# Splitting the second expert matrix into two parts, one tile ahead

## The chip, the cores and the metric

One core of a Trainium2 chip runs the whole program. Times are device microseconds (us) of that core; several runs of the same program give a median. One execution was recorded by the hardware profiler, and all rows of the trace come from it.

## What is computed

Attention with a block mask (4 x 8 heads, 576 tokens, 64 wide) gives x of 2304 tokens by 512. A dense layer follows, and then a layer of 8 experts, in which each token goes to one expert or to none. What matters here is that last layer:

```python
def _moe2_ref(x, w_skip, w_gate, w1, w2):
    do_compute = x @ w_skip > 0
    out = x.copy()
    xc = x[do_compute]
    logits = xc @ w_gate
    e_idx = np.argmax(logits, axis=1)
    ...
    for e in range(E):          # E = 8, w1[e] is 512 x 1024, w2[e] is 1024 x 512
        mask = e_idx == e
        h = np.maximum(xc[mask] @ w1[e], 0.0)
        y[mask] = gate_w[mask, None] * (h @ w2[e])
    out[do_compute] = xc + y
```

## The kernel before

Attention comes first, the dense layer overlaps its end, and the expert layer is the last stage. Tokens are sorted by expert into lists in DRAM. A tile is 128 tokens of one expert: their rows are gathered, turned by TensorE (turn_x, L881), multiplied with the expert's first matrix (two halves of 512 columns, four chunks of rows each), passed through relu (ScalarE), turned again (turn_h), multiplied with the second matrix (8 chunks of rows, summed in one bank, py), scaled and added to x by VectorE (finisher, L966 to L974: the tile yo) and scattered to the output by GpSimd. The number of tokens decides at run time how many tiles an expert has: further tiles stand in nested conditional blocks (tc.If, L1132), and expert 7 stands in one as a whole (L1117). The instructions of a block are ordered by a scheduler that lists what is ready by its own estimate of time; each engine then works in that order. tc.keep_in_program_order puts an instruction behind the one that was written before it on the same engine.

Two forms of product are in use. Expert 0 (expert_tile, L926) has its weights and its inputs split into a rounded part (hi, type float32r) and the rest (lo), and computes a product as three: hi*hi, hi*lo, lo*hi (products, L893). ScalarE or VectorE makes the rounded part, VectorE or GpSimd subtracts (split_piece, L859). The raw weights come in pieces of 128 rows by 512 columns through places of the pool CV (raw holds two pieces, cv2 and cv3 one, three places each), 12 pieces ahead (load_piece, L842). Experts 1 to 7 (expert_tile32, L976) multiply float32 with float32 directly: mm1 at L984, mm2 at L987, the copy of turned h at L997. Their two matrices are loaded by SP into one of four pairs of places (load_expert, L816), up to four experts ahead. Expert 0's first tile is computed early, beside the routing of the last tokens; its second (the call with filled, L1131) follows at about 700 us, while SP loads the lists of all experts (L1093 to L1096).

Of the kernel before, what the change touches and what calls it, by code (L numbers as in the profile page):

```python
# [346 lines left out]
def attention_moe_kernel(  # L347
# [468 lines left out]
    def load_expert(e):  # L816

        if e >= E:
            return
        k_ = (e - 1) % 4  # L820
        if k_ < 3:
            x, y = ((wo_at[0], wo_at[1]), (wi_at[2], wo_at[2]), (wi_at[0], wi_at[1]))[k_]
            a, b = ((WA if t < 2 else WB).tile([128, 2, 4 * 512], F32, name=f"wbt{t}").rearrange("p i w -> p (i w)") for t in (x, y))
            a, b = a.rearrange("p (c w) -> p c w", w=F2), b.rearrange("p (c k w) -> p c k w", k=2, w=D)
        else:
            a, b = (C.tile([128, ND, HALF], F32, name=f"xT{i}") for i in range(2))
            a, b = a[:, :, 0:F2], b[:, :, 0 : 2 * D].rearrange("p c (k w) -> p c k w", k=2)
        for c in range(ND):
            nc.sync.dma_start(a[:, c], w1[e, c * 128 : (c + 1) * 128])
        for c in range(ND):  # L830
            nc.sync.dma_start(b[:, c], w2[e, c * 256 : (c + 1) * 256].rearrange("(k p) w -> p k w", p=128))
        weights[e] = [a[:, c] for c in range(ND)], [b[:, f // 2, f % 2] for f in range(NF2)]

# [65 lines left out]
    def places(own=False):  # L899

        bank = lambda nm, *shape: ps3.tile([128, *shape], F32, name=nm, tag="ps")
        return dict(hh=M3.tile([128, NF2, 128], F32R, name="hh", bufs=1),
                    hl=M3.tile([128, NF2, 128], F32R, name="hl", bufs=1),
                    ph=[bank("ph3", 512) for _ in range(2)],
                    py=psx.tile([128, 512], F32, name="py", bufs=1) if own else bank("py", 512),
                    pt=lambda: bank("pt", 4, 128), hs=lambda f: M3.tile([128, 512], F32, name="hs"),
                    yo=lambda: M3.tile([128, 512], F32, name="yo"))

# [16 lines left out]

    def expert_tile(lx, ahead=(), at=None, begin=run_all, between=None):  # L926

# [19 lines left out]
        begin(m1[0])  # L947
        relu(0)
        run_all(m1[1][:9] if between else m1[1][:7])
        if between:  # L950
# [5 lines left out]
        turn_h(1)  # L956
        run_all(m2[4:7])
        if between:
            between[1]()
# [15 lines left out]

    def expert_tile32(e, hw, lx, ahead=(), at=None):  # L976

        a, b = weights[e]
        at = at or places()
        ph, py = at["ph"], at["py"]  # L980
        h = {}

        def mm1(f, c):
            tc.keep_in_program_order(nc.tensor.matmul(ph[f], lx["xw"][:, c], a[c][:, f * 512 : f * 512 + 512], start=(c == 0), stop=(c == ND - 1)))  # L984

        def mm2(f):
            tc.keep_in_program_order(nc.tensor.matmul(py, hw[:, f], b[f], start=(f == 0), stop=(f == NF2 - 1)))  # L987

        def relu(f):
            h[f] = at["hs"](f)  # L990
            nc.scalar.activation(out=h[f], in_=ph[f], func=AF.Relu)

        def turn_h(f):
            pt = at["pt"]()
            for c in range(4):
                tc.keep_in_program_order(nc.tensor.transpose(pt[:, c], h[f][:, c * 128 : (c + 1) * 128], ident))
            nc.vector.tensor_copy(hw[:, 4 * f : 4 * f + 4], pt)  # L997

        for c in range(ND):
            mm1(0, c)  # L1000
        relu(0)
        for c in range(2):
            mm1(1, c)
        turn_h(0)
        for c in range(2, ND):
            mm1(1, c)
        relu(1)
        for f in range(2):
            mm2(f)
        turn_h(1)  # L1010
        for f in range(2, 6):
            mm2(f)
        run_all(ahead)
        for f in range(6, NF2):
            mm2(f)
        return finisher(lx, at, py)
# [76 lines left out]
    with tc.issue_after(end.ins):  # L1093
        for k_ in (2, 1, 0, 3):
            load_lists(lall[k_], lambda l: l.rearrange("(e n) c -> n e c", e=E)[k_ * 128 : (k_ + 1) * 128], nc.sync)
            find(lall[k_])  # L1096
    for e in (1, 2):
        load_expert(e)
    p2.close()
# [3 lines left out]
    xgs.insert(4, xgf[1])  # L1103
    xts = [[M3.tile([128, ND, 128], F32R, name=f"xt{i}{j}", bufs=1) for j in range(2)] for i in range(2)]
    xts = [xtf[0], xts[0], xtf[1], xts[1]]
    fourth = lane(lall[3], 0, xgs[0], xts[2])
    xws = [CV.tile([128, ND, 128], F32, name=nm, bufs=3) for nm in ("cv2", "cv2", "cv3", "cv3")]
    hw = [CV.tile([128, NF2, 128], F32, name="raw", bufs=3) for _ in range(2)]
    firsts = [lane32(lall[0], e, xgs[e % 4], xws[e % 2]) for e in range(E)]
    for lx in (firsts[1], fourth, firsts[2], firsts[3]):  # L1110
        gather(lx)
    for e in range(E):
        ahead1 = [lambda: turn_x(firsts[e + 1])] if e + 1 < E else []
        some = ExitStack()
        if e:
# [3 lines left out]
            gather(second)  # L1119
            finish = expert_tile32(e, hw[0], firsts[e], ahead1, at=places(True))  # L1120

# [5 lines left out]

        tile_of = (lambda *a: expert_tile32(e, hw[1], *a)) if e else expert_tile

        def more(k_, lx):  # L1130
            filled = e == 0 and k_ == 1  # L1131
            with nullcontext() if filled else tc.If(nreg[e] > 128 * k_):  # L1132
                if k_ == 1 and not filled:
                    turn_x(lx)
                if k_ < KS:
                    ahead = []
                    nx = later(k_ + 1)
                    if k_ + 1 < KS:
                        if nx is not fourth:
                            gather(nx)  # L1140
                        ahead = [lambda: turn_x(nx)]
                    finish = tile_of(lx, ahead + (ahead1 if filled else []))
                    finish()
# [50 lines left out]
```

## Time and profile before

| | us |
|---|---|
| median of 3 runs | 867.64 (866.53 to 868.01) |
| the profiled execution, its own time | 869.34 |
| span from first to last instruction in it | 867.6 |
| TensorE busy in the span | 799.5 (92%) |
| VectorE, ScalarE, GpSimd busy | 524.2, 399.0, 354.0 |

The profile names the engines PE (TensorE products), PEld (TensorE's loading of the fixed operand, which overlaps), DVE (VectorE), ACT (ScalarE), POOL (GpSimd) and SP (the engine that issues most transfers); a q behind the name is the engine's sequencer. A row of the timeline gives start, duration, engine, line of the kernel, operation, tile written<-tiles read and a count; in brackets stand the idle time before it and what ended it. "issue" there means that nothing the profile shows was waited for. Both types of product are called f32 in it.

### The profile page before, as it was taken

How to read it: one execution, taken by the hardware profiler on the slowest of the kernel's cores; microseconds unless marked ns; L12 is line 12 of the kernel's file. 1: busy time of each engine (PE TensorE's matmuls, PEld its weight loads, DVE VectorE, ACT ScalarE, POOL GpSimd, SP SyncE). 2: the span in 40 equal slices, each digit the busy share in tenths (PEclk: the TensorE clock that was granted, in tenths of full speed). 3: DMA queues.
4: the chain of work that ended last, by engine and by line, in shares of the span. 5: the costliest groups of instructions: out<-in, count | busy, mean ns of one | idle time of the engine just before them, and what ended most of it. 6: DMA issues, size and time to landing. Idle time of an engine off the chain costs nothing. (4 is left out here: it accounts for less than half of the span.)

```text
span 867.6 us, 12388 instructions
## 1 busy us (share of the span) xinstructions
PE 799.5 (92%) x4100; PEld 657.4 (76%) x4100; DVE 524.2 (60%) x1122; ACT 399.0 (46%) x909; POOL 354.0 (41%) x427
## 2 busy tenths in 40 slices
PE   6688999989999999987999999999999979989995
PEld 4577787979888788876899888898998758544442
DVE  6786888877968984489719798558222722111111
ACT  5786887877778774565422222222232412101110
POOL 3665554453545564455432544423315341010210
PEclk9899999999999998998999999999999989999998
DMA  6564753474341143543521523113036761693920
GB/s 168 138 180 109 192 124 82 108 190 129 72 106 42 40 165 121 167 156 130 169 73 73 170 69 128 37 73 110 3 116 206 271 95 37 230 398 140 320 60 7
DMA packets 114653, 112.89 MB, mean 130 GB/s; under 512 B 76718, under 2 KB 79790, under 8 KB 114562
## 3 DMA queue, kind: packets, MB, share of 16 engines
q1 hardware_dynamic: 106386, 95.72, 36.4%
q0 software_dynamic: 8176, 16.06, 6.2%
q8 instruction: 44, 0.72, 0.3%
q14 instruction: 47, 0.39, 0.1%
HBM read 81.23 MB, written 22.70 MB: 120 GB/s over the span
## 5 line engine op out<-in xcount | busy, mean ns | idle before, releaser
L438 PE MATMUL ph<-xT,wbt 128*128 128x384 f32 x864 | 168.7, 342 | 0.7 <-ACT cv L480 0.7
L438 PEld LDWEIGHTS ph<-xT,wbt 128*128 128x128 f32 x864 | 155.2, 191 | 8.4 <-ACT cv L480 1.1
L430 POOL TENSOR_TENSOR gl<-u,gh 128x384 fp32r<-128x384 f32 x72 | 80.2, 1115 | 154.3 <-ACT gh L429 129.5
L438 PE MATMUL acc<-wbt,gh 128*128 128x512 f32 x432 | 133.3, 398 | 7.6 <-ACT cv L405 4.9
L185 POOL TENSOR_SCALAR P<-P,stat 128x128 f32<-128x128 f32 (+2 forms) x144 | 78.9, 568 | 76.4 <-DVE stat L183 54.6
L429 DVE TENSOR_TENSOR u<-ph,u 128x384 f32<-128x384 f32 x72 | 39.6, 550 | 97.4 <-ACT u L428 94.7
L438 PEld LDWEIGHTS acc<-wbt,gh 128*128 128x128 f32 x432 | 80.0, 188 | 21.1 <-ACT cv L405 5.1
L429 ACT CAST gh<-u 128x384 fp32r<-128x384 f32 x72 | 36.9, 512 | 104.7 <-PE acc L438 49.3
L438 PE MATMUL acc<-wbt,gl 128*128 128x512 f32 x216 | 82.1, 396 | 0.0
L428 ACT ACTIVATE u<-ph 128x384 f32<-128x384 f32 x72 | 35.2, 489 | 83.1 <-PE ph L438 75.2
L285 PE MATMUL pv<-ph,vs 128*128 128x320 f32 (+4 forms) x280 | 70.7, 323 | 2.7 <-DVE ph L239 1.6
L161 PE MATMUL sp<-wbt 128*128 128x128 f32 (+2 forms) x192 | 58.2, 382 | 12.4 <-DMA wbt<-wbt 4.9
L236 PE MATMUL pt<-ident,P 128*128 128x128 f32 x400 | 62.6, 283 | 6.2 <-ACT P L174 2.5
L438 PE MATMUL ph<-xT,wia 128*128 128x384 f32 x288 | 58.9, 351 | 3.4 <-DVE cv L429 2.1
L409 POOL TENSOR_TENSOR cv<-cv,cv 128x512 int32<-128x512 int32 x32 | 45.5, 1424 | 32.7 <-DVE cv L408 21.8
L285 PEld LDWEIGHTS pv<-ph,vs 128*128 128x128 f32 x280 | 51.2, 192 | 8.9 <-DVE ph L239 2.5
L438 PE MATMUL po<-woa,gA 128*128 128x512 f32 x216 | 56.4, 407 | 0.5 <-ACT cv L480 0.5
L648 DVE CUSTOM_DVE_ANT_0 xlast<-x,raw 128x512 f32<-128x512 f32 x72 | 56.7, 834 | 0.0
L236 PEld LDWEIGHTS pt<-ident,P 128*128 128x128 f32 x400 | 47.0, 143 | 11.9 <-ACT P L174 3.1
L438 PEld LDWEIGHTS ph<-xT,wia 128*128 128x128 f32 x288 | 51.7, 196 | 4.5 <-DVE cv L429 2.4
L243 DVE TENSOR_TENSOR pl<-pt,ph 128x512 fp32r<-128x512 f32 (+2 forms) x84 | 50.9, 624 | 5.2 <-ACT ph L242 4.2
L438 PEld LDWEIGHTS po<-woa,gA 128*128 128x128 f32 x216 | 41.2, 195 | 9.0 <-ACT cv L480 0.9
(244 smaller groups left out, 1537.7 us busy)
## 6 DMA issues: line engine op xcount, KB each, us to landing
wbt<-in_moe_w_dram SPq DMA_DIRECT2D x48, 512.0 KB, 6.9
wbt<-wbt SPq DMA_DIRECT2D x60, 144.0 KB, 2.5
raw<-in_moe_w_in_dram SPq DMA_DIRECT2D x16, 512.0 KB, 4.1
raw<-in_moe_w_out_dram SPq DMA_DIRECT2D x16, 512.0 KB, 3.7
xTd<-xT POOLq DMA_DIRECT2D x4, 1152.0 KB, 8.0
part_d<-cv SPq DMA_DIRECT2D x18, 256.0 KB, 2.1
x<-part_d SPq DMA_DIRECT2D x6, 768.0 KB, 4.6
xT<-xTd POOLq DMA_DIRECT2D x6, 768.0 KB, 6.9
```

The source lines that it names most:

```text
L161: nc.tensor.matmul(o_, st()[a][h][:, rows : rows + m], st()[b][:, h, c : c + w], start=(i == 0), stop=(i == 1))
L185: nc.gpsimd.tensor_scalar(out=P, in0=P, scalar1=rs[:, i : i + 1], scalar2=1.0, op0=ALU.mult, op1=ALU.mult)
L236: nc.tensor.transpose(o, src, self.ident)
L243: nc.vector.tensor_tensor(out=dl, in0=s_, in1=dh.bitcast(F32), op=ALU.subtract)
L285: nc.tensor.matmul(box["pv"][:, c0:N], v, box[t][:, i, h, cs], start=(jc == 0 and t == "ph"), stop=(jc == runs[-1][0] and t == parts[-1]))
L409: nc.gpsimd.tensor_tensor(out=w, in0=w, in1=low, op=ALU.add)
L428: nc.scalar.activation(out=u, in_=ph, func=AF.Copy, scale=0.01)
L429: return [nc.vector.tensor_tensor(out=u, in0=ph, in1=u, op=ALU.max), nc.scalar.copy(gh, u), nc.gpsimd.tensor_tensor(out=gl, in0=u, in1=gh. ...
L430: nc.gpsimd.tensor_tensor(out=gl, in0=u, in1=gh.bitcast(F32), op=ALU.subtract)]
L438: nc.tensor.matmul(ps, x, y, start=first and m == 0, stop=last and m == 3 * n - 1)
L648: nc.vector.tensor_tensor_reduce(out=junk, in0=x2[:, t], in1=wrow[j], scale=1.0, scalar=0.0, op0=ALU.mult, op1=ALU.add, accum_out=box["L"] ...
```

## The change

The second matrix of experts 1 to 7 is split like expert 0's. Its raw pieces come through the places of CV, 12 pieces ahead (load_later), and are split during the first tile of the expert before (split_later), a few in four places of that tile, eight in expert 0's second tile for expert 1. The split matrix goes to one of two places in turn: the third pair of the dense layer's weights for odd experts, expert 0's own place for even ones. load_expert now loads the first matrix alone, into one of four places. In the tile, h is split as in expert 0 (ScalarE copies, VectorE subtracts), and the second matrix takes 24 products instead of 8. The first stays float32. The turned x gets places of its own, since CV's are taken, and the result yo has one place instead of two.

```diff
--- before.py
+++ after.py
@@ -817,19 +817,44 @@
 
         if e >= E:
             return
-        k_ = (e - 1) % 4
-        if k_ < 3:
-            x, y = ((wo_at[0], wo_at[1]), (wi_at[2], wo_at[2]), (wi_at[0], wi_at[1]))[k_]
-            a, b = ((WA if t < 2 else WB).tile([128, 2, 4 * 512], F32, name=f"wbt{t}").rearrange("p i w -> p (i w)") for t in (x, y))
-            a, b = a.rearrange("p (c w) -> p c w", w=F2), b.rearrange("p (c k w) -> p c k w", k=2, w=D)
-        else:
-            a, b = (C.tile([128, ND, HALF], F32, name=f"xT{i}") for i in range(2))
-            a, b = a[:, :, 0:F2], b[:, :, 0 : 2 * D].rearrange("p c (k w) -> p c k w", k=2)
+        t = (wo_at[0], wo_at[1], wi_at[0], wi_at[1])[(e - 1) % 4]
+        a = (WA if t < 2 else WB).tile([128, 2, 4 * 512], F32, name=f"wbt{t}").rearrange("p i w -> p (i w)").rearrange("p (c w) -> p c w", w=F2)
         for c in range(ND):
             nc.sync.dma_start(a[:, c], w1[e, c * 128 : (c + 1) * 128])
-        for c in range(ND):
-            nc.sync.dma_start(b[:, c], w2[e, c * 256 : (c + 1) * 256].rearrange("(k p) w -> p k w", p=128))
-        weights[e] = [a[:, c] for c in range(ND)], [b[:, f // 2, f % 2] for f in range(NF2)]
+        if e % 2:
+            b = [wbt[t].rearrange("p i (f w) -> p (i f) w", w=D) for t in (wi_at[2], wo_at[2])]
+            b = [[x[:, f] for f in range(NF2)] for x in b]
+        else:
+            b = w2buf
+        weights[e] = [a[:, c] for c in range(ND)], b
+
+    later_raws = {}
+
+    def load_later(i):
+
+        e, f = divmod(i, NF2)
+        e += 1
+        if e >= E:
+            return
+        nm = tags[i % AHEAD]
+        n = 2 if nm == "raw" else 1
+        t = CV.tile([128, n, 512], F32, name=nm, bufs=3)
+        for k_ in range(n):
+            later_raws[i + k_] = t[:, k_]
+        nc.sync.dma_start(t, w2[e, f * 128 : (f + n) * 128, :].rearrange("(n p) w -> p n w", p=128))
+
+    def split_later(e):
+
+        def step(f):
+            i = (e - 1) * NF2 + f
+            (hi, lo), r = (x[f] for x in weights[e][1]), later_raws.pop(i)
+            tc.keep_in_program_order(nc.scalar.copy(hi, r))
+            nc.vector.tensor_tensor(out=lo, in0=r, in1=hi.bitcast(F32), op=ALU.subtract)
+            nm = tags[i % AHEAD]
+            if nm != "raw":
+                load_later(i + AHEAD - (nm is None))
+
+        return [lambda f=f: step(f) for f in range(NF2)] if e < E else []
 
 
     tags = ("raw", None, "cv2", "cv3") * 3
@@ -904,7 +929,7 @@
                     ph=[bank("ph3", 512) for _ in range(2)],
                     py=psx.tile([128, 512], F32, name="py", bufs=1) if own else bank("py", 512),
                     pt=lambda: bank("pt", 4, 128), hs=lambda f: M3.tile([128, 512], F32, name="hs"),
-                    yo=lambda: M3.tile([128, 512], F32, name="yo"))
+                    yo=lambda: M3.tile([128, 512], F32, name="yo", bufs=1))
 
     def places_early():
 
@@ -923,7 +948,7 @@
                     pt=lambda: bank("acc1", 4, 128),
                     yo=lambda: CV.tile([128, 512], F32, name="cv2", bufs=3))
 
-    def expert_tile(lx, ahead=(), at=None, begin=run_all, between=None):
+    def expert_tile(lx, ahead=(), at=None, begin=run_all, between=None, fill=()):
 
         a, b = w1buf, w2buf
         at = at or places()
@@ -946,6 +971,7 @@
 
         begin(m1[0])
         relu(0)
+        run_all(fill[:4])
         run_all(m1[1][:9] if between else m1[1][:7])
         if between:
             between[0]()
@@ -955,6 +981,7 @@
         run_all(m2[:4])
         turn_h(1)
         run_all(m2[4:7])
+        run_all(fill[4:])
         if between:
             between[1]()
         run_all(m2[7:18])
@@ -973,18 +1000,16 @@
 
         return finish
 
-    def expert_tile32(e, hw, lx, ahead=(), at=None):
-
-        a, b = weights[e]
+    def expert_tile32(e, lx, ahead=(), at=None, fill=()):
+
+        a, (bh, bl) = weights[e]
         at = at or places()
-        ph, py = at["ph"], at["py"]
-        h = {}
+        ph, py, hh, hl = at["ph"], at["py"], at["hh"], at["hl"]
+        m2 = products(py, [(hh[:, c], hl[:, c]) for c in range(NF2)], list(zip(bh, bl)))
+        h, fill = {}, list(fill)
 
         def mm1(f, c):
             tc.keep_in_program_order(nc.tensor.matmul(ph[f], lx["xw"][:, c], a[c][:, f * 512 : f * 512 + 512], start=(c == 0), stop=(c == ND - 1)))
-
-        def mm2(f):
-            tc.keep_in_program_order(nc.tensor.matmul(py, hw[:, f], b[f], start=(f == 0), stop=(f == NF2 - 1)))
 
         def relu(f):
             h[f] = at["hs"](f)
@@ -994,25 +1019,31 @@
             pt = at["pt"]()
             for c in range(4):
                 tc.keep_in_program_order(nc.tensor.transpose(pt[:, c], h[f][:, c * 128 : (c + 1) * 128], ident))
-            nc.vector.tensor_copy(hw[:, 4 * f : 4 * f + 4], pt)
-
+            nc.scalar.copy(hh[:, 4 * f : 4 * f + 4], pt)
+            nc.vector.tensor_tensor(out=hl[:, 4 * f : 4 * f + 4], in0=pt, in1=hh[:, 4 * f : 4 * f + 4].bitcast(F32), op=ALU.subtract)
+
+        def some():
+            run_all(fill[:2])
+            del fill[:2]
+
+        some()
         for c in range(ND):
             mm1(0, c)
         relu(0)
+        some()
         for c in range(2):
             mm1(1, c)
         turn_h(0)
         for c in range(2, ND):
             mm1(1, c)
         relu(1)
-        for f in range(2):
-            mm2(f)
+        some()
+        run_all(m2[:5])
         turn_h(1)
-        for f in range(2, 6):
-            mm2(f)
+        run_all(m2[5:16])
+        some()
         run_all(ahead)
-        for f in range(6, NF2):
-            mm2(f)
+        run_all(m2[16:])
         return finisher(lx, at, py)
 
     seq = [(n, f) for a, b in cuts for n in order[:3] for f in range(a, b)]
@@ -1094,18 +1125,19 @@
         for k_ in (2, 1, 0, 3):
             load_lists(lall[k_], lambda l: l.rearrange("(e n) c -> n e c", e=E)[k_ * 128 : (k_ + 1) * 128], nc.sync)
             find(lall[k_])
-    for e in (1, 2):
-        load_expert(e)
+    load_expert(1)
+    for j in range(AHEAD):
+        if tags[j]:
+            load_later(j)
+    load_expert(2)
     p2.close()
     ps3 = ctx.enter_context(tc.tile_pool(name="ps3", bufs=7, space=PSUM))
     M3 = ctx.enter_context(tc.tile_pool(name="m3", bufs=2))
     xgs = [xgf[0]] + [M3.tile([128, D], F32, name=f"xg{i}", bufs=1) for i in range(1, 5)]
     xgs.insert(4, xgf[1])
-    xts = [[M3.tile([128, ND, 128], F32R, name=f"xt{i}{j}", bufs=1) for j in range(2)] for i in range(2)]
-    xts = [xtf[0], xts[0], xtf[1], xts[1]]
+    xts = [xtf[0], None, xtf[1], [M3.tile([128, ND, 128], F32R, name=f"xt{j}", bufs=1) for j in range(2)]]
     fourth = lane(lall[3], 0, xgs[0], xts[2])
-    xws = [CV.tile([128, ND, 128], F32, name=nm, bufs=3) for nm in ("cv2", "cv2", "cv3", "cv3")]
-    hw = [CV.tile([128, NF2, 128], F32, name="raw", bufs=3) for _ in range(2)]
+    xws = [M3.tile([128, ND, 128], F32, name=f"xw{i}", bufs=1) for i in range(4)]
     firsts = [lane32(lall[0], e, xgs[e % 4], xws[e % 2]) for e in range(E)]
     for lx in (firsts[1], fourth, firsts[2], firsts[3]):
         gather(lx)
@@ -1117,7 +1149,7 @@
                 some.enter_context(tc.If(nreg[e] > 0))
             second = lane32(lall[1], e, xgs[4], xws[2])
             gather(second)
-            finish = expert_tile32(e, hw[0], firsts[e], ahead1, at=places(True))
+            finish = expert_tile32(e, firsts[e], ahead1, at=places(True), fill=split_later(e + 1))
 
         def later(k_):
             if e == 0 and k_ == 3:
@@ -1125,7 +1157,7 @@
             L, n = (lall[k_], e) if k_ < KS else (llate, 0)
             return (lane32 if e else lane)(L, n, xgs[4 + (k_ + 1) % 2], (xws if e else xts)[2 + (k_ + 1) % 2])
 
-        tile_of = (lambda *a: expert_tile32(e, hw[1], *a)) if e else expert_tile
+        tile_of = (lambda *a: expert_tile32(e, *a)) if e else expert_tile
 
         def more(k_, lx):
             filled = e == 0 and k_ == 1
@@ -1139,7 +1171,7 @@
                         if nx is not fourth:
                             gather(nx)
                         ahead = [lambda: turn_x(nx)]
-                    finish = tile_of(lx, ahead + (ahead1 if filled else []))
+                    finish = tile_of(lx, ahead + (ahead1 if filled else []), **(dict(fill=split_later(1)) if filled else {}))
                     finish()
                     more(k_ + 1, nx)
                 else:
```

## Rows read from the trace of the kernel before

**Rows 1.** Table of stretches: PE, PEld, DVE, ACT, POOL busy; clock, DMA share, GB/s.

```profile
744.50:760.00 15.50, 14.86 (x44) 7.17 (x44) 2.48 (x4) 1.57 (x3) 1.99 (x2) 1.00 0.94 343
760.00:776.90 16.90, 15.11 (x44) 7.17 (x44) 2.56 (x4) 1.57 (x3) 3.90 (x4) 1.00 1.03 400
...
825.00:840.60 15.60, 15.30 (x46) 7.17 (x44) 2.56 (x4) 1.57 (x3) 1.96 (x2) 1.00 0.13 35
```

**Rows 2.** Timeline, the tile of expert 5 and the start of the next.

```profile
825.85 5.39 PE L984 MATMUL ph<-wbt,cv 128*128 128x512 f32 x12 [0.30 <-PEq L1132]
...
833.23 1.88 PE L987 MATMUL py<-wbt,raw 128*128 128x512 f32 x4
...
833.49 0.60 ACT L991 ACTIVATE hs<-ph 128x512 f32<-128x512 f32 x1 [3.27 <-PE ph L984]
...
834.95 0.60 PE L996 MATMUL pt<-ident,hs 128*128 128x128 f32 x4
...
835.38 3.60 PE L987 MATMUL py<-wbt,raw 128*128 128x512 f32 x8
835.59 0.69 DVE L997 COPY raw<-pt 128x512 f32<-128x512 f32 x1 [3.18 <-PE pt L996]
...
839.26 1.88 PE L987 MATMUL py<-wbt,raw 128*128 128x512 f32 x4
...
841.44 5.39 PE L984 MATMUL ph<-wbt,cv 128*128 128x512 f32 x12 [0.30 <-PEq L1132]
```

**Rows 3.** The line of the second matrix: count, min/median/max ns, first and last start.

```profile
L987 PE MATMUL py<-wbt,raw x96: 592/592/595, 752.5 to 856.1; 128*128 128x512 f32 x96
...
L987 PE MATMUL py<-xT,raw x16: 592/592/595, 817.6 to 825.0; 128*128 128x512 f32 x16
```

**Rows 4.** Timeline, products of split parts in expert 0's later tiles.

```profile
719.52 4.58 PE L897 MATMUL ph<-wbt,xt 128*128 128x512 f32 x19
...
743.98 0.40 PE L897 MATMUL py<-xT,hl 128*128 128x512 f32 x1
```

**Rows 5.** By line: splits of expert 0's weights (L867, L868) and of h.

```profile
L867 ACT CAST xT<-raw x4: 605/614/617, 647.0 to 678.2; 128x512 fp32r<-128x512 f32 x4
...
L868 DVE TENSOR_TENSOR xT<-raw,xT x4: 679/884/1753, 647.6 to 683.3; 128x512 fp32r<-128x512 f32 x4
...
L868 POOL TENSOR_TENSOR xT<-cv,xT x2: 1287/1287/1287, 653.2 to 679.4; 128x512 fp32r<-128x512 f32 x2
...
L944 ACT CAST hh<-pt 128x512 fp32r<-128x512 f32 x2 | 1.2, 586 | 6.8 <-PE pt L943 6.8
...
L945 DVE TENSOR_TENSOR hl<-pt,hh 128x512 fp32r<-128x512 f32 x2 | 1.4, 692 | 2.8 <-ACT hh L944 2.8
```

**Rows 6.** Branches of PE's sequencer behind experts 1, 5 and 6: ns, start.

```profile
L1132 PEldq COMPARE_BRANCH  x1: 6153/6153/6153, 755.7 to 755.7; - x1
...
L1132 PEldq COMPARE_BRANCH  x1: 1660/1660/1660, 836.4 to 836.4; - x1
...
L1132 PEldq COMPARE_BRANCH  x1: 3343/3343/3343, 852.0 to 852.0; - x1
```

**Rows 7.** Timeline, the starts of experts 2 and 3, and expert 2's scatters.

```profile
762.22 5.39 PE L984 MATMUL ph<-wbt,cv 128*128 128x512 f32 x12 [1.79 <-PEq L1132]
...
794.67 5.39 PE L984 MATMUL ph<-wbt,cv 128*128 128x512 f32 x12 [0.95 <-DVEq L1132]
794.79 1.01 POOL L970 DMA_INDIRECT out_dram<-yo,la1ix  x1 [27.69 <-DVEq L1132]
...
803.21 1.01 POOL L970 DMA_INDIRECT out_dram<-yo,la0ix  x1 [4.86 <-DMA out_dram<-yo,la1ix]
```

**Rows 8.** Timeline, lists and hl in expert 0's second tile.

```profile
709.21 0.26 DVE L614 TENSOR_REDUCE la3li<-la3l 128x32 f32<-128x96 f32 x1 [1.61 <-DMA la3l<-list]
...
709.68 0.69 DVE L945 TENSOR_TENSOR hl<-pt,hh 128x512 fp32r<-128x512 f32 x1
...
710.43 0.80 PE L897 MATMUL py<-xT,hl 128*128 128x512 f32 x1 [3.47 <-DVE hl L945]
```

## The prediction

> **What bounds the kernel now.** I read the page first: TensorE is busy for most of the span, but that is an average, so I went to the stretches. The change lives in the expert stage, from about 700 us to the end. The table of stretches [rows 1] shows what limits it there: in the tile of expert 5 PE is busy 15.30 of 15.60 us, while VectorE, ScalarE and GpSimd work 2.6, 1.6 and 2.0 us. DMA is full in the first two stretches of the single-precision experts and nearly idle in the later one, and PE's share does not care. So experts 1 to 7 are bound by TensorE, and a change is worth what it takes off that engine, minus the waits it puts in front of it.
>
> The timeline of expert 5's tile [rows 2] gives the anatomy. From its first product (825.85) to the next tile's (841.44) is 15.59 us. A run of 8 records takes 3.60 us and a run of 4 takes 1.88, so one record costs (3.60 - 1.88) / 4 = 0.430 us and the last one shows 0.59. Four transposes cost 835.38 - 834.95 = 0.43 us. The second matrix has 8 products in the code, yet the line has 96 + 16 records [rows 3]. One tile has 16 of them (4 + 8 + 4 in rows 2), so 112 records are 7 tiles: experts 1 to 6, one of them (expert 2) with two; expert 7 is skipped. A float32 product is thus two records, 0.86 us.
>
> The price of the other form stands in expert 0's tiles [rows 4]: 19 products of split parts with the same 128x512 shape take 4.58 us, the last one 0.40, hence (4.58 - 0.40) / 18 = 0.232 us each. Three of them, which replace one float32 product, cost 0.70 us.
>
> **The change, part by part.**
>
> *Second matrix.* Removed per tile: 16 x 0.430 = 6.88 us. Added: 24 x 0.232 = 5.57. That is -1.31 us a tile, and -9.2 us over 7 tiles. First matrix (16 records), three groups of transposes and the gap between tiles stay: the new tile is 15.59 - 1.31 = 14.3 us.
>
> *Splitting.* Each tile gets 8 splits: a ScalarE copy, 0.62 us, and a VectorE subtraction, 0.69 to 0.88 [rows 5]. ScalarE worked 1.57 us in the tile [rows 1] and gets 8 x 0.62 and two casts of 0.59 on top: 7.7 us. VectorE worked 2.56; its two copies of 0.69 turn into two subtractions of 0.69, and 8 x 0.69 come on top: 8.1 us. Both fit under 14.3, so the work is hidden by PE; without that cover it would cost 5 us a tile.
>
> *The chain of h.* A VectorE copy (0.69) becomes a ScalarE cast and then a VectorE subtraction (0.59 + 0.69). Is the second half in time? Counted from the tile's start: m2 starts at 7.38, five products bring us to 8.54, four transposes to 8.97, and the first product with a low part of the second half is nine products later, at 11.06. The copy starts 0.64 after the transposes (835.59 - 834.95), so the cast runs 9.18 to 9.77 and the subtraction to 10.46: 0.60 us spare. The third pair of splits stands behind the second relu, which ends at 8.24; its copies end at 9.48, so the cast moves by 0.30, and the subtractions (8.86 to 10.17) move the last one to 10.86. Still 0.20 spare. With subtractions of 0.88, the median of the splits, it ends at 11.31: 0.25 late. The longest, 1.75, would make it 2.0 late; but it stands among splits of expert 0, where GpSimd subtracts as well [rows 5], and here GpSimd only issues transfers. Bounds 0 and 7 x 0.25 = 1.8; I take +0.7, nearer to the 0.69 that the same operation on h takes.
>
> *Loads.* SP issues four loads fewer with an expert and six smaller ones out of the splits. An expert still needs 4 MB, 10.5 us at the 400 GB/s of rows 1, under 14.3; the pieces of w2 are asked for 12 pieces ahead, more than a tile before their split. What waits behind a late one is ScalarE's queue, since a copy stands behind the instruction traced before it: the relu or the cast behind it, and then PE. I put 0 here, covered by that distance; a load 2 us late would cost PE up to 2 us, once.
>
> *Branches between tiles.* PE's sequencer reaches the branch that skips an expert's further tiles early: in expert 5 at 836.4, while the last product ends at 839.26 + 1.88 = 841.14 [rows 2, 6]. The 1.66 us of the branch is hidden under 4.7 us of queued work: 13 records, of which 4 are transposes. After the change the same 13 records last 0.43 + 9 x 0.232 + 0.17 = 2.7 us. The branch after expert 1 took 6.15 us and already showed: PE idled 1.79 us in front of expert 2 [rows 7]. With 2.0 us less cover it shows 2.0 more. The 1.66 stays hidden. The 3.34 is in front of the skipped expert 7, where PE has nothing to do. Bounds: -1.8 (a short branch there) and +2.0 with 5 x (3.34 - 2.7) = 3.2 on top, 5.2; I take +2.0.
>
> [...]
>
> *One place for the result (yo).* With two tiles, expert 2 finishes the second first. Its scatter was issued at 794.79 and the next one waited for it until 803.21 [rows 7]. With one place VectorE, too, must wait until about 803.2 before it writes the other result, and ends at 803.95. The product bank of expert 3's first tile is free only then, and its m2 wants it at 794.67 + 7.38 = 802.05: 1.9 us late. If VectorE's order puts this before expert 3's first h (due 7.84 after its start), two pairs of subtractions and that of h follow: 9.28 + 5 x 0.69 = 12.7, 4.9 late. If the scatter lands sooner, since only half of the weights load then: 0. Bounds 0 and 4.9; I take +1.0.
>
> *Expert 0's second tile* now carries 8 splits. Here VectorE is already the late engine: it waits for a list by DMA until 709.21, hl comes at 709.68, and PE sits idle 3.47 us [rows 8]. Four subtractions are traced ahead of hl: up to 4 x 0.69 = 2.8 us more, and 1 MB of w2 that is loaded among the lists could hold them 2.6 us at 400 GB/s. If the new order lets hl go first, the 3.47 vanish. Bounds -3.5 and +5.4; I take +1.5, since two of 0.69 fit into the 1.61 us that VectorE idles before the last list.
>
> *Other edits.* Own tiles for x, and the hl and hh that exist already: no instruction more, no wait that the profile shows.
>
> Sum: -9.2 + 0.7 + 2.0 + 1.0 + 1.5 = -4.0 us. The profiled execution took 869.34 us, 1.7 above the median of the runs; it would take 865.3, and the median run 867.64 - 4.0 = 863.6.
>
> **Rivals.**
>
> *Branches decide (slower).* Place: the six boundaries behind experts 1 to 6's tiles (expert 2's two tiles end in one). Price: a branch of 6.15 us with 2.7 us of cover shows 3.45 us; six of them less the 1.8 of now is +18.9, with the other terms (-9.2 + 3.2 = -6.0) +12.9: 880.5. It costs all of the gain from a mean branch of about 2.7 + 7.8 / 6 = 4.0 us on (7.8 is 6.0 and the 1.8 of now). For it: rows 6 have both 3.34 and 6.15, and DMA is busier now in all tiles. Against: 1.66 was usual. Chance 0.10.
>
> *VectorE's queue eats it (no change).* A subtraction of h that stands behind waiting work costs PE up to the upper bounds, 1.8 in the tiles, 4.9 at yo and 2.5 in expert 0, instead of 0.7, 1.0 and 1.5: -9.2 + 2.0 + 9.2 = +2.0; halfway there, -1.0: 866.6. For it: the queue is in order, and rows 8 show it held by DMA already. Against: 6 us of VectorE are free in each tile. Chance 0.15.
>
> *The old stall goes too (faster still).* hl of expert 0's second tile ahead of the lists: -9.2 + 0.7 + 2.0 + 1.0 - 3.5 = -9.0: 858.6. Chance 0.12.
>
> *Not what it says.* If PE does the split products at 0.43 us, as a half clock would, m2 costs 24 x 0.43 = 10.3 instead of 6.88: +24 us, 892. Rows 1 grant 1.00 in all three stretches; chance 0.02.
>
> **How the numbers follow.** The forecast has 0.61. This measurement tells about 0.2%, 1.7 us, from no change: faster is below 865.9. The forecast and the third rival are faster, as is a little of the second: 0.74. Same: most of the second and a little of the forecast, 0.14. Slower: the first, the fourth: 0.12. The range reaches from the third rival, 858.0, past the second to 868.6; the dear ends of branches and of yo lie beyond.
>
> **What would show it.** Tile of expert 5 from first product to next at 14.3 us, m2 records 0.232 apart; ScalarE and VectorE near 8 us in it. The gap before expert 2's first product near 3.8 us. In expert 3, m2 starting about 1 to 2 us late behind yo. In expert 0's second tile, hl at about 711. The prediction is wrong if tiles show waits for hl, if several branches pass 3 us, or if the lists come in another order.

## The result and the profile after

The change made the kernel slower: 874.22 us (873.24 to 875.88, 5 runs) against 867.64 (866.53 to 869.59, 5 runs), a ratio of 1.0067 [1.0042, 1.0093]. The forecast was 863.6 with a range up to 868.6; it was wrong in sign and the time lies outside its range.

The profiled execution took 875.85 us, its span 874.1 us. Lines of its page (the slices are fortieths of the span):

```profile
span 874.1 us, 12712 instructions
...
PE 797.9 (91%) x4156; PEld 670.8 (77%) x4156; DVE 560.5 (64%) x1178; ACT 436.6 (50%) x979; POOL 355.9 (41%) x427
...
PEclk9999999999999999998999999999999979999998
```

TensorE has lost 1.6 us of its busy time, not the 9.2 that the new products save, and one late slice is at seven tenths of the clock. The table of stretches answers to [rows 1]. The first stretch is what remains of expert 0; each of the others holds one tile of experts 1 to 6, those from 759.00 and 776.00 both of expert 2:

```profile
core 0: us, PE busy (x) PEld busy (x) DVE busy (x) ACT busy (x) POOL busy (x), PEclk, DMA share, GB/s
697.00:744.57 47.57, 41.56 (x181) 32.63 (x181) 14.22 (x28) 13.10 (x24) 8.82 (x9) 0.89 0.48 126
744.57:759.00 14.43, 14.02 (x52) 8.61 (x52) 7.41 (x13) 6.52 (x13) 1.98 (x2) 1.00 0.96 358
759.00:776.00 17.00, 14.34 (x40) 7.93 (x41) 6.33 (x11) 6.57 (x12) 4.21 (x4) 0.80 0.95 331
776.00:793.90 17.90, 17.06 (x70) 10.95 (x68) 3.42 (x7) 3.73 (x8) 0.00 (x0) 1.00 0.18 59
793.90:814.50 20.60, 16.85 (x51) 10.59 (x52) 7.69 (x13) 6.71 (x13) 4.65 (x4) 0.83 0.70 249
814.50:829.00 14.50, 14.20 (x54) 8.66 (x53) 7.54 (x12) 6.93 (x13) 3.27 (x3) 1.00 0.85 298
829.00:847.50 18.50, 15.99 (x54) 9.24 (x52) 7.92 (x13) 6.95 (x13) 2.29 (x2) 0.91 0.38 115
847.50:862.50 15.00, 14.00 (x52) 8.65 (x52) 7.88 (x13) 6.94 (x13) 2.29 (x2) 1.00 0.10 32
```

The tiles of experts 1, 4 and 6 are what was forecast: PE works 14.0 to 14.2 us in each, VectorE 7.4 to 7.9 and ScalarE 6.5 to 6.9. Those from 759.00, 793.90 and 829.00 are 2 to 6 us longer, and in exactly these the granted clock is 0.80 to 0.91. (The one from 776.00 begins in the late end of the tile before; its own tile takes 14.02 us.) The starts of the tiles on PE's timeline, with expert 3's inner waits, say what came before:

```profile
761.66 8.34 PE L1012 MATMUL ph<-wbt,xw 128*128 128x512 f32 x12 [3.07 <-PEq L1164]
...
794.47 5.39 PE L1012 MATMUL ph<-wbt,xw 128*128 128x512 f32 x12 [0.95 <-DVEq L1164]
802.99 0.71 PE L922 MATMUL py<-wbt,hh 128*128 128x512 f32 x2 [0.97 <-DVE yo L996]
805.90 0.79 PE L922 MATMUL py<-wbt,hl 128*128 128x512 f32 x1 [2.21 <-DVE hl L1023]
815.25 5.39 PE L1012 MATMUL ph<-wbt,xw 128*128 128x512 f32 x12 [0.30 <-PEq L1164]
831.33 7.11 PE L1012 MATMUL ph<-wbt,xw 128*128 128x512 f32 x12 [2.09 <-DVE xT L852]
847.75 5.39 PE L1012 MATMUL ph<-wbt,xw 128*128 128x512 f32 x12 [0.67 <-PEq L1164]
```

Twelve records take 5.39 us at full clock. Behind an idle of 3.07 us they take 8.34, behind one of 2.09 us 7.11: the granted clock is 0.50 instead of 1.00 from 760.78 to 767.60 us and from 832.46 to 835.87, and that costs nearly as much again as the idle, 2.95 and 1.72 us. Expert 3 starts at full clock and stalls inside. VectorE's timeline shows with what:

```profile
802.09 0.75 DVE L996 SCALAR_TENSOR_TENSOR yo<-py,la0li,xg 128x512 f32<-128x512 f32 x1 [7.78 <-PE ph L1012]
802.76 1.28 DVE L852 TENSOR_TENSOR xT<-raw,xT 128x512 fp32r<-128x512 f32 x2
803.96 1.29 DVE L852 TENSOR_TENSOR xT<-cv,xT 128x512 fp32r<-128x512 f32 x2
805.16 0.68 DVE L1023 TENSOR_TENSOR hl<-pt,hh 128x512 fp32r<-128x512 f32 x1
```

VectorE stood 7.78 us before expert 2's second yo, whose only place was free when the earlier scatter had landed, at 801.87 us; then four subtractions of the next expert's matrix went ahead of hl, for which PE waited. The name in the bracket of the first row is not the cause: this yo reads py, la0li and xg.

The branches of PE's sequencer that answer to [rows 6], behind experts 1, 3, 4 and 5 and over expert 7 (ns, start):

```profile
L1164 PEldq COMPARE_BRANCH  x1: 6044/6044/6044, 755.3 to 755.3; - x1
...
L1164 PEldq COMPARE_BRANCH  x1: 3547/3547/3547, 810.4 to 810.4; - x1
...
L1164 PEldq COMPARE_BRANCH  x1: 427/427/427, 826.0 to 826.0; - x1
...
L1164 PEldq COMPARE_BRANCH  x1: 3642/3642/3642, 843.8 to 843.8; - x1
...
L1194 PEldq COMPARE_BRANCH  x1: 4985/4985/4985, 862.1 to 862.1; - x1
```

From expert 1's first product to the end of the span the kernel before took 122.42 us, the changed one 129.49, 7.07 more: seven tiles -9.0 (14.0 instead of 15.29 from first to last product), the gap before expert 2 +1.28 and its half clock +2.95, expert 3's stall with its half clock +6.46 (20.48 us for a tile of 14.02), the gap before expert 5 +1.79 and its half clock +1.72, the gap before expert 6 +0.37, and the tail behind the last product +1.48. These sum to +7.05. Expert 0's second to fourth tiles take 2.6 us more (47.54 against 44.95), and everything before them, which the change leaves alone, was 3.2 us shorter in this execution; 7.07 + 2.6 - 3.2 is the 6.5 us between the two spans.

### The profile page after: what moved, and what is told of

The parts are those of the page before. It is cut to its first block, busy times and chain, and to the rows that moved or that the text cites. A ratio compares the mean times of both kernels' runs of the same rounds, so it can differ in the third digit from the quotient of the medians.

```text
span 874.1 us, 12712 instructions
## 1 busy us (share of the span) xinstructions
PE 797.9 (91%) x4156; PEld 670.8 (77%) x4156; DVE 560.5 (64%) x1178; ACT 436.6 (50%) x979; POOL 355.9 (41%) x427
## 5 line engine op out<-in xcount | busy, mean ns | idle before, releaser
L1012 PE MATMUL ph<-wbt,xw 128*128 128x512 f32 x112 | 55.6, 643 | 8.1 <-PEq L1164 4.6
```

## The experiments

All kernels start from the changed one unless the text says otherwise; "before" ran beside each on the same chip (867.8 to 869.0 us), and ratios are to it. "Stretch" is the time from expert 1's first product to the end of the span in the profiled execution.

**Finish first.** Each tile's yo and scatter are put ahead of the further tiles' block:

```diff
-        more(1, second)
         if e:
             finish()
+        more(1, second)
+        if e:
             load_expert(e + 4)
```

> The changed kernel (median 874.2 us), with one line moved: the first tile of an expert is scaled and scattered before the block of its further tiles instead of behind it, so that yo and the bank py are free long before expert 3. Theory A (the single place of yo holds VectorE until expert 2's scatter has landed, PE then idles 0.97 and 2.21 us in expert 3, and the half clock that follows costs 3.3 us more): the tile of expert 3 falls from 20.5 to about 14.0 us, and the kernel to about 867.7 us. Rival B (the eight splits in VectorE's queue are the cause, and hl would be late behind them in any case): only the 0.97 us come back, about 873 us.

Measured: 868.21 us, 1.0026 [0.999, 1.0061]; stretch 122.59, 6.9 less, which is a sum, above all of these: expert 3's stall is gone (6.5), expert 2's half clock did not come (2.95), and expert 4 now starts 1.5 us later and at half clock (1.7). In expert 3's tile hl is made in time, and yo waits for its own product alone:

```profile
798.05 0.68 DVE L1023 TENSOR_TENSOR hl<-pt,hh 128x512 fp32r<-128x512 f32 x1
...
802.17 0.75 DVE L996 SCALAR_TENSOR_TENSOR yo<-py,la0li,xg 128x512 f32<-128x512 f32 x1 [1.02 <-PE py L922]
```

The tile takes 14.02 us: the stall of 6.5 us was the order and the one place of yo. Finishing first has a price, about 1 us of gap before experts 5 and 6 (0.95 and 1.02, "DVEq L1164"), as each block now waits for VectorE.

**One further tile only, in both kernels.** The third and later tiles of experts 1 to 7 are left out of the code (their rows would not be computed; here no expert has a third tile):

```diff
             filled = e == 0 and k_ == 1
+            if e and k_ > 1:
+                return
```

> The changed kernel without the third and further tiles of experts 1 to 7, and without their loop, in the code; no expert but expert 0 has more than two tiles here, so no work that runs is left out, but PE's branch jumps over one tile instead of four. Theory A (the gaps of 3.07, 2.09 and 0.67 us before experts 2, 5 and 6, and the long end, are PE waiting for its instructions): the branches fall below 0.5 us, the gaps to 0.3, the half clock after them goes (4.7 us), the end gets 1 to 5 us shorter: 860 to 864 us. Rival B (the gaps are waits for splits or transfers that only look like branches): the gaps stay, 873 to 875 us.

> The kernel before (median 867.6 us) with the same cut of code that does not run. Theory A: PE idles 1.5 us less before expert 2, and the 3.6 us branch over expert 7 at the end shrinks by up to 3.3: 863 to 865 us. Rival B (no branch sets the time of the kernel before, the end is set by the last scatter): 866 to 868 us.

Measured: the changed kernel 857.05 us (4 runs), 0.9865 [0.979, 0.994]; the kernel before 862.76, 0.9923 [0.989, 0.996]. No product, copy or transfer that runs was taken away, only code that is jumped over. Branches behind experts 1 and 5 in the changed kernel:

```profile
L1166 PEldq COMPARE_BRANCH  x1: 354/354/354, 759.6 to 759.6; - x1
...
L1166 PEldq COMPARE_BRANCH  x1: 212/212/212, 831.5 to 831.5; - x1
```

From expert 1's first to the last product, first the changed kernel, then the kernel before, both with the short code:

```profile
748.84:849.17 100.33, 98.30 (x368) 61.00 (x368) 47.34 (x77) 44.16 (x84) 18.68 (x17) 1.00 0.67 236
```

```profile
746.22:855.49 109.27, 107.25 (x312) 50.73 (x312) 17.62 (x29) 11.33 (x22) 16.71 (x17) 1.00 0.63 226
```

The difference, 8.94 us, is the forecast's 9.2 for the split, with the clock at 1.00 in both. Between the two spans 6.3 of it are left, since expert 0's last three tiles took 2.0 us more (45.61 against 43.64) and the work ahead of them 0.7; the medians differ by 5.7. So the length of these two branches, 6.04 and 3.64 us in the changed kernel, comes from the code that they jump over, and the kernel before paid about 5 us for it too.

**The same in a kernel for every count.** From the third tile on, experts 1 to 7 use the loop that was there from the fifth on; in the first run with finishing first, in the second without:

```diff
+        ks = 2 if e else KS
...
-                if k_ < KS:
+                if k_ < ks:
...
-                    with tc.For_i(KS, (nreg[e] + 127) // 128, 1) as i:
+                    with tc.For_i(ks, (nreg[e] + 127) // 128, 1) as i:
```

> The changed kernel with the finish of the first tile ahead of the further tiles, and with the third and later tiles of experts 1 to 7 in the loop instead of written out, so that PE's branch jumps over two tiles instead of four; it can do all that the changed kernel can. [...] Rival (any jump out of order costs its 3.4 to 6 us): about 867 us, as with the finish alone.

> The changed kernel with only the code that is jumped over made shorter: experts 1 to 7 have their third and later tiles in the loop that was there for the fifth and later ones, so one skipped tile and one loop body lie behind each expert instead of three skipped tiles and a loop body. Theory A (what is jumped over sets the branches): the branches behind experts 1, 3, 5 and 7 take 0.2 to 0.5 us instead of 3.5 to 6.0, the gaps before the tiles 0.3 to 0.5, no half clock behind expert 1; the wait of yo for expert 2's scatter stays (it depends on the scatter's landing) or shrinks with the freer bus. From expert 1's first product to its last product 102 to 107 us (117.2 in the changed kernel), the time 858 to 863. Theory B (branches cost what they cost by being taken, wherever they go): gaps and time as in the changed kernel, 874.

Measured: 860.08 us, 0.9896 [0.9866, 0.9926], inside the 856 to 861 that the author estimated from short branches and the 6.5 us of expert 3, and 859.9, 0.9907 [0.9877, 0.9936]. All branches that jump take 0.17 to 0.54 us. With the loop, expert 2's second tile no longer gathers and turns the rows of a third; with that this tile takes 13.6 us instead of 14.0. In the second run, expert 3's stall is still there:

```profile
797.40 0.71 PE L922 MATMUL py<-wbt,hh 128*128 128x512 f32 x2 [0.66 <-ACT hs L1016]
800.31 0.51 PE L922 MATMUL py<-wbt,hl 128*128 128x512 f32 x1 [2.20 <-DVE hl L1023]
```

The two losses are thus separate. Finishing first takes 2.2 us off the time from expert 1 to the last product (103.46 against 105.63) and puts 3.3 on the tail (11.33 against 8.01), so it wins nothing here.

**Two places for yo.** The fourth place of the turned x, which only third and later tiles use, makes room:

```diff
-                    yo=lambda: M3.tile([128, 512], F32, name="yo", bufs=1))
+                    yo=lambda: M3.tile([128, 512], F32, name="yo"))
```

> The changed kernel with one thing undone: the row of outputs yo again has two places (the place of a turned row that only skipped third tiles use is given up for it). Theory A (expert 3's stall is the single place of yo, not the queue of VectorE's subtractions by itself): the wait of line 996 for expert 2's scatter is gone, expert 3's tile takes 14.0 us instead of 20.5, no half clock follows it, and from expert 1's first product to the end the profiled execution takes about 123 us (129.5 in the changed kernel), the time about 868. It must do so without the 0.7 to 1.1 us of gap that finishing first put before each tile, so the gaps before the tiles stay those of the changed kernel (3.1 behind expert 1, 2.1 or less behind expert 4). Theory B (the four subtractions ahead of hl cost it): PE still idles about 2.2 us before the third products of expert 3, and the time falls by no more than 2 us.

Measured: 869.35 us, 1.001 [0.998, 1.004]; stretch 124.98, so 4.5 less and not 6.5. Expert 3's stall is gone, but its end met a branch that the stall had covered:

```profile
L1164 PEldq COMPARE_BRANCH  x1: 6032/6032/6032, 810.5 to 810.5; - x1
```

```profile
816.85 7.09 PE L1012 MATMUL ph<-wbt,xw 128*128 128x512 f32 x12 [3.08 <-PEq L1164]
```

In the changed kernel that branch took 3.55 us and showed 0.30.

**The loads beside the branch behind expert 1.** Three times the first matrices of experts 3 and 4 (4 MB) were to be loaded later: traced behind expert 1, traced behind expert 2, and held with an order after expert 2's first products:

> The changed kernel, but the first matrices of experts 3 and 4 (4 MB) are asked for behind expert 1 instead of ahead of it; both are needed only 30 us later. Theory A, second half (the branch behind expert 1 takes 6.0 us instead of about 3.5 because its instructions queue behind weights): the branch takes about 3.6 us, PE idles about 1 instead of 3.07 us before expert 2, and the half clock in its first tile (3.0 us) goes: about 869 us. Rival (the traffic of weights does not touch the branch): 6 us again, 874 us.

> The changed kernel, with the first matrices of experts 3 and 4 asked for behind expert 2's tiles. (The run before this one put them behind expert 1; SP jumps over that block at once and asked for them at the same moment as ever, so it tested nothing.) SP reaches the new place only after it has issued the pieces of expert 2's first tile, so that only 2 MB of pieces load during expert 1's tile. Theory A, second half (instructions queue behind weights): the branch behind expert 1 takes 3.4 to 4 instead of 6.0 us, PE idles about 1 us before expert 2, and the kernel gains 2 to 5 us on the changed one. Rival (the length of this branch has nothing to do with the traffic): 6.0 us again.

> The changed kernel with the loads of experts 3's and 4's first matrices held until expert 2's first four products have been issued (the two earlier tries left them where they were). This takes 4 MB off the bus in the stretch in which PE's branch behind expert 1 runs. Theory A (the branch behind expert 1 is longer than those behind experts 3, 5 and 7 because its instructions are fetched beside full queues, the bus at 103% there): it takes 3.4 to 4.0 us instead of 6.0, the gap before expert 2 falls from 3.1 to below 1 us, no half clock follows, and from expert 1's first product to the end it is 4 to 5 us less, the time about 869. [...] If the loads come too late for expert 3, PE waits for wbt ahead of expert 3's first products, and only the branch's length is read from the run.

Measured: 875.24, 875.32 and 873.87 us, 1.0071, 1.0083 and 1.0069. None of them tested what it was made for: SP asked for the eight loads at 743 to 752 us each time, whether they were written later or ordered behind TensorE's products, and the branch took 6.0 to 6.1 us. They are three more executions of the same work. The fourth ordered them behind a load on SP's own queue, in expert 2's tile:

```diff
...
+        if e == 2 and weights[3][0] is None:
+            with tc.issue_after(ld[0].ins):
+                load_expert(3)
+                load_expert(4)
...
```

> The changed kernel with the loads of experts 3's and 4's first matrices (4 MB) put behind the second load of a piece in expert 2's tile on SP's own queue, so that SP can't ask for them before expert 2's tile has begun; in the three earlier tries SP asked for them at 743 to 752 us all the same. In the stretch of PE's branch behind expert 1 the bus then carries only expert 2's pieces and rows (below half of its share, 1.03 in the changed kernel). Theory A (that branch takes 6 us because its instructions come beside full queues): 3.4 to 4.0 us, as behind experts 3, 5 and 7, and the gap before expert 2 below 1 us. [...] Expert 3 may wait for its matrix; the run is read by the branch, not by its time (868 to 876).

Measured: 868.88 us, 1.0023 [0.9992, 1.0053]. The stretch from 754 to 762 us, in the changed kernel, whose branch stands from 755.3 to 761.3, and then in this one, where it stands from 752.9 to 757.6; below it this one's branch and expert 2's start:

```profile
754.00:762.00 8.00, 4.93 (x23) 3.77 (x22) 3.56 (x6) 2.26 (x5) 0.27 (x1) 0.92 1.04 400
```

```profile
754.00:762.00 8.00, 6.30 (x22) 3.48 (x20) 2.50 (x5) 1.84 (x4) 3.26 (x3) 1.00 0.76 235
```

```profile
L1171 PEldq COMPARE_BRANCH  x1: 4644/4644/4644, 752.9 to 752.9; - x1
```

```profile
757.90 5.39 PE L1015 MATMUL ph<-wbt,xw 128*128 128x512 f32 x12 [1.70 <-PEq L1171]
```

The branch lies between theory A and the changed kernel: with DMA less busy (0.67 of its share during the branch, against 1.04) the branch takes 4.64 us instead of 6.04, not the 3.4 to 4.0 of theory A, over a jump of the same length. The gap shrinks by 1.37 us, and the half clock behind it (2.95) does not come; the latter alone says little, as the last section shows.

**Splits later, and all repairs together.** All eight splits of expert 0's second tile go behind the second turn of h; first with finishing first and the cut code, then with the loop from the third tile and two places for yo, a kernel for every count:

```diff
-        run_all(fill[:4])
...
-        run_all(fill[4:])
+        run_all(fill)
```

> The changed kernel with one further tile in the code of experts 1 to 7 (their third and later tiles and the loop, which do not run here, are left out), with the finish of the first tile ahead, and with the eight splits in expert 0's second tile all behind the turning of the second half of h. Against the run with only the cut (857.0 us): theory A says that the first four splits cost expert 0's tile what PE idled there beyond the list (3.69 + 0.92 us against 3.3 to 3.5 in kernels without splits) and some half clock, so 1 to 3 us less, 854 to 856 us. Rival (the lists alone set that stall): 857 us.

> All three repairs that the runs point to, in a kernel that still does every count of rows: the shorter code behind each expert (loop from the third tile), yo with two places, and all eight subtractions and copies of expert 1's second matrix in expert 0's second tile behind the turn of h's second half instead of half of them ahead of it. Theory A (the three losses are separate and add): tiles of 14.0 us with gaps of 0.3 to 0.5, no half clock from expert 1 on, 100.3 us from expert 1's first to the last product, expert 0's last three tiles 44 to 45.5 us, tail 8 to 11; the time 854 to 859, below every kernel with finishing first (860.1). Theory B (the clock falls or a wait comes up elsewhere): not below 860.

Measured: 859.5 us, 0.990 [0.987, 0.993], above what was expected, as finishing first left gaps of 1.1 us and a tail of 9.63 instead of 8.05; and 853.81, 0.9841 [0.9809, 0.9873], the fastest of all. Its tiles of experts 1 to 6:

```profile
746.83 5.39 PE L1011 MATMUL ph<-wbt,xw 128*128 128x512 f32 x12 [0.54 <-PEq L1165]
761.13 5.39 PE L1011 MATMUL ph<-wbt,xw 128*128 128x512 f32 x12 [0.30 <-PEq L1165]
776.02 5.42 PE L1011 MATMUL ph<-wbt,xw 128*128 128x512 f32 x12 [0.46 <-ACT xw L912]
790.24 5.39 PE L1011 MATMUL ph<-wbt,xw 128*128 128x512 f32 x12 [0.64 <-PEq L1165]
804.65 5.39 PE L1011 MATMUL ph<-wbt,xw 128*128 128x512 f32 x12 [0.40 <-PEq L1165]
...
833.45 5.39 PE L1011 MATMUL ph<-wbt,xw 128*128 128x512 f32 x12 [0.40 <-PEq L1165]
```

No start is idle for more than 0.64 us and all run at full clock. The later splits added nothing that can be told: expert 0's last three tiles take 45.45 us here and 45.62 without.

## Why the prediction was wrong, step by step

*Second matrix: right.* -9.2 was forecast; the tiles show -9.0, and the two kernels with short code -8.94. *Splitting and the chain of h: right, at the good end.* VectorE and ScalarE work 7.4 to 7.9 and 6.5 to 6.9 us, and outside expert 3 no tile waits for hl: 0 instead of +0.7. (A slip that changes nothing: two subtractions of 0.69 from 8.86 on end at 10.24, not 10.17, which leaves 0.13 us spare instead of 0.20.)

*Branches between tiles: the step that failed.* The step took each branch's duration from the kernel before, let 2.0 us come up before expert 2, and said that the 1.66 stays hidden. Before expert 2 the gap grew by 1.28: the cover fell from 4.8 to 3.3 us, not to 2.7. The other branches did not keep their durations: behind expert 5 it is 3.64 instead of 1.66, and behind expert 3 it is 3.55 (4.77 and 6.03 in the two kernels in which that tile isn't stalled), where the kernel before has

```profile
L1132 PEldq COMPARE_BRANCH  x1: 848/848/848, 805.2 to 805.2; - x1
```

The packets on the instruction queue q8 (46 of them, 0.75 MB, on the changed kernel's page) show what stands beside such a duration. Each of these branches ends 1.3 to 1.5 us after a fetch of 16 KB, itself about 1 us long, has landed. In the kernel before, behind experts 3, 4 and 5, that fetch had begun 0.6 to 1.5 us before the branch, and only its rest shows in 0.85, 1.22 and 1.66 us. In the changed kernel it begins 1.0 to 1.2 us after the branch has begun, and behind expert 1 3.5 us after it (2.2 in the fourth run on the loads). So, by these times, the 1.66 us that the step carried over was the rest of a fetch already under way. Why the fetch begins later against the branch in the changed kernel no run isolates.

Behind expert 4 the branch is short (0.43), but PE starts 2.09 us late. The row names VectorE's subtraction as releaser; in five other kernels with this code the work so named was done 0.2 to 0.7 us before PE started. In that stretch stands one fetch of instructions (queue, kind: packets, MB, share of 16 engines):

```profile
q8 instruction: 1, 0.02, 2.1%
```

It lands 1.46 us before PE's next product, and in the five other kernels such a fetch lands 1.4 to 1.5 us before it, the interval that stands behind the long branches too; in the kernel with short code the gap is 0.40. That PE waited for this fetch is argued from these times; no run isolates it. Gaps (+3.4) with the tail (+1.5) exceed the forecast's 2.0, and would still be inside its bound of 5.2.

*What no term held: the clock.* Each gap of the two and the stall in expert 3 was followed by a stretch at a granted clock of 0.50 (from 760.78 to 767.60, 832.46 to 835.87 and 805.15 to 811.98 us): 2.95 + 1.72 + about 3.3 (expert 3: 6.46 less its idle of 0.97 and 2.21) = 8.0 us. It is no fixed price: in the three runs that left the loads where they were the half clock comes to 6.5, 2.2 and 6.4 us, though all are slower than the kernel before. The forecast had read in [rows 1] that the clock stood at 1.00 and kept it; [rows 8] held the idle of 3.47 us with which it had fallen once (0.50 from 709.21 to 716.04 us), and that was not used. With the half clock the branches, the late start and the tail cost 3.4 + 4.7 + 1.5 = 9.6 in this execution instead of 2.0.

*One place for yo: right mechanism, wrong size.* The step described it as it came: VectorE stands before yo until the scatter has landed, at 802.09 (803.2 forecast), PE's first wait ends at 802.99, and subtractions of the next matrix go ahead of hl. It was bounded by 4.9 and taken at 1.0. Its waits are 0.97 and 2.21, together 3.2; with the half clock, which the step did not hold, it cost 6.5.

*Expert 0's second tile: +1.5 forecast, +2.6 measured.* PE idles 3.86 us before hl, as it did before (3.47), and then another 1.58; the half clock (0.50 from 706.16 to 716.40 us), which the kernel before has here too (from 709.21 to 716.04), costs, by difference, about 0.8 us more:

```profile
707.65 0.79 PE L922 MATMUL py<-xT,hl 128*128 128x512 f32 x1 [3.86 <-DVE hl L970]
...
708.76 1.14 ACT L851 CAST wbt<-cv 128x512 fp32r<-128x512 f32 x2 [5.97 <-DMA cv<-in_moe_w_dram]
...
709.81 0.59 ACT L963 ACTIVATE hs<-ph 128x512 f32<-128x512 f32 x1
...
710.45 0.90 PE L968 MATMUL pt<-ident,hs 128*128 128x128 f32 x3 [1.58 <-ACT hs L963]
```

The second wait is the one named under loads: a piece that came late holds ScalarE's queue, and the relu behind the casts is late. It was asked for at 704.34 us, behind the lists, and landed at 708.74, so for expert 1's pieces the distance that was to cover the loads was not there. In the profiles of the other kernels with the same code in this place the three tiles take 44.4 to 46.8 us, so 2.6 is the upper end.

*Loads* cost nothing in the tiles of experts 1 to 6, but the tail grew: expert 7's branch takes 4.99 us instead of 3.56, and the last scatter lands 3.9 us after its issue where it took 2.5. The end waits for that scatter, in both kernels 7.3 us from its landing. Two fetches of 16 KB of instructions run beside it, where there was one; with the short code, where one runs, it lands after 2.3 us. That the fetches delay it is argued, not tried.

The rival "Branches decide" had the right place: in the changed kernel the branches take 3.4 to 6.0 us over the long code, with a fetch of 16 KB in each that lands 1.4 to 2.1 us before its end, except behind expert 4 (0.43), and 0.2 to 0.5 over the short. The rival asked for six such gaps and got two. The second rival, VectorE's queue, came true in one of its three places, at yo; in expert 0 it was ScalarE's queue that cost, and the rival's 2.5 us for that place is worked out from no row.

## What to carry to other kernels

Make the tile shorter and what was hidden under its last products can show, as it did before expert 2 (a gap of 3.07 us instead of 1.79): for each branch, scatter or list that ends just in time now, work out what cover is left. Price the idle of TensorE that a change may bring with the half clock that can follow it, here 2.2 to 8.0 us in four executions of the same work. And take no branch's duration from the kernel before without asking what it was waiting for. Code that is never run had a price here when it was jumped over: moving the rare tiles into a loop took the changed kernel from 0.7% above the kernel before to 0.9% below it, and giving yo its second place back (with the later splits) to 1.6% below. The kernel before gains 0.8% itself when that code is left out, so only about half of the 1.6% comes from the split.

## What the runs showed of the hardware

The branches of PE's sequencer took 0.2 to 0.5 us over one tile, with a loop body or without; over three tiles and a loop body 0.85 to 6.15 in the kernel before and 3.4 to 6.0 in the changed kernel (6.62 behind expert 1 with two places for yo), but 0.43 behind expert 4, where PE stood 2.09 us later instead. In the traces of these two kernels a branch of more than 0.6 us ends 1.3 to 1.5 us after a fetch of 16 KB on q8 has landed (2.1 once, over expert 7, where two fetches overlap). Behind expert 1 it took 6.04 us with DMA at 1.04 of its share during the branch, and 4.64 at 0.67 in the fourth run on the loads; behind expert 5, at 0.03, it still took 3.64. Nor did an idle's length alone decide in these runs whether the clock fell: before expert 2 it fell behind 3.07 us of idle in the changed kernel, and stayed full behind 3.07 in the second try to load later and behind 3.14 with finishing first, where expert 4's start lost it behind 1.81:

```profile
758.27 5.39 PE L1012 MATMUL ph<-wbt,xw 128*128 128x512 f32 x12 [3.14 <-PEq L1164]
```

Executions also differ ahead of the change: expert 0's second tile began between 696.1 and 703.7 us in the profiled kernels, whose code up to there does the same, which is why the stretches behind it, and not single spans, were compared.
